# The layer norm's short steps moved off GpSimd, the residual sum as a ScalarE pass, and q weights permuted by their load

## The chip, the cores and the metric

The kernel runs on one core of a Trainium2 chip. The metric is the device time of one launch in microseconds (us); lower is better. Most quoted times are medians of several runs. A run counts as slow when it lies more than 1.5% above the fastest of the same kernel; medians and ranges list all runs. The engines are called PE (TensorE), DVE (VectorE), ACT (ScalarE), POOL (GpSimd) and SP (the sync engine, which here only issues DMAs). The profile counts sixteen DMA engines for the queues of the core.

## The reference

The input is x, 2048 tokens of width 640, in bf16. Cut to what matters:

```python
xn  = (x - mean(x)) / sqrt(var(x) + 1e-5)              # layer norm, per token
q, k, v = split(xn @ wqkv)                             # 32 heads of 20 columns
phi = lambda t: where(t > 0, t + 1, exp(t)) + 1e-6
kv  = phi(k)^T v ; z = sum(phi(k))                     # per head, over all tokens
A   = (phi(q) @ kv) / (phi(q) . z + 1e-6) @ wo
idx = top 8 tokens of xn @ w_r                         # routing
y   = (silu(xn[idx] @ w_gate) * (xn[idx] @ w_up)) @ w_down * sigmoid(r[idx])
out = x + A + xn + scatter_add(idx, y)                 # note the x + xn
```

## The kernel before

The work falls into three stages. In the first, 16 tiles of 128 tokens go through the norm, a transpose (by DMA; the first two tiles by PE), the K projection (`K`, with the router column), `phi` (`PHa`, `PHb`) and the Gram matrix (`G`, xn^T phi(k)). The second computes q, multiplies the weights together and routes eight tokens through the expert block. The third forms the 16 output tiles. The parts that the change and the argument touch, shortened; `...` marks a cut:

```python
def ln_stats(t, part=None):                      # DVE: two halves, then mean and variance
    ... dve.bn_stats(...) ; dve.bn_stats(...) ; dve.bn_aggr(out=mvs[t][:], in_=sts[t][:])

def ln_mid(t, on_act=True):
    ...
    pool.tensor_scalar(out=nm[:], in0=mv[:, 0:1], scalar1=-1.0, ..., op0=ALU.mult)
    act.activation(c[:], XX[:, t, 1, :], AF.Identity, bias=nm[:])          # c = x - mean
    pool.tensor_scalar(out=t2[:], in0=mv[:, 1:2], scalar1=EPS_BF16, ..., op0=ALU.add)
    pool.tensor_tensor(out=s[:], in0=t2[:], in1=halfc[:], op=ALU.pow)      # sqrt(var + eps)

def ln_xn(t):
    dve.reciprocal(sr[:], s[:])
    dve.tensor_scalar(out=XX[:, t, 0, :], in0=c[:], scalar1=sr[:], ..., op0=ALU.mult)

def tr_dma(t):                                   # xn -> xnT, by the DMA engines
    sp.dma_start_transpose(xnT[:, :, t * P : (t + 1) * P], XX[:, t, 0, :])

def xpx(t, eng=None):                            # x + xn in place, read by the outputs
    (eng or pool).tensor_tensor(out=XX[:, t, 1, :], in0=XX[:, t, 1, :], in1=XX[:, t, 0, :], op=ALU.add)

for t in range(T):
    K(t)                                         # PE, reads xnT of tile t
    PHb(t - 1)                                   # DVE: pk = min(ek, 1) + rk
    ln_xn(t + 2) ; tr_dma(t + 2)                 # two tiles ahead
    ln_stats(t + 3)
    if t in dve_extra: perm_q(dve_extra[t])      # two DVE copies, tiles 6 to 10
    PHa(t)                                       # ACT: ek = exp, rk = relu
    ln_mid(t + 3)
    G(t - 1)                                     # PE, reads pk of tile t - 1
    ...
    if 7 <= t: xpx(t)                            # tiles 0 to 6 follow in stage 2
    loads(t)                                     # weights for stages 2 and 3, all on the sync queue
```

`loads` spreads the later weights over the loop: q (0.8 MB) at tiles 4 and 5, o at 6 and 7, gate (2 MB) at 6 to 10, up (2 MB) at 11 to 15, v at 12 and 13; down (2 MB) comes after the loop.

## Time and profile before

| | us |
|---|---|
| median of all runs (lowest, highest) | 143.65 (143.02 to 143.92) |
| span of the profiled run | 142.3 |
| stage 1, to the first q matmul | 72.0 |
| stage 2, from there to the first output matmul | 38.5 |
| stage 3, from there to the end | 31.8 |

The page's busy shares of the kernel before; each row of digits is the span in 40 slices of 3.56 us, in tenths (PEclk is the granted PE clock, DMA the mean busy share of the 16 DMA engines):

```profile
PE 118.6 (83%) x952; PEld 65.5 (46%) x952; DVE 99.7 (70%) x216; ACT 68.8 (48%) x166; POOL 58.6 (41%) x99
PE   6669887887757756669999999894999999999970
POOL 5264468775556775599000047999000000000000
PEclk9977999999999999999999999999689999999999
DMA  4954656695994564398449200000000022222222
```

Counted from 0, PE has its gaps in slices 0 to 17, the stage-1 loop. In slice 27 it pauses and in 28 and 29 it runs at a lower clock, just after POOL worked again (PE is idle from 97.5 to 99.5 us, and its granted clock is 0.50 from 101 to 104 us).

The chain of waits of the kernel before, over one turn of the loop (start us, length us, what):

```profile
43.57 1.24 DVE XX L165
44.81 0.40 DVE stats L138
45.21 0.40 DVE stats L140
45.63 0.22 DVE mv L141
45.93 0.24 POOL nm L152
46.25 0.82 POOL t L157
47.14 0.58 POOL s L158
48.02 1.24 DVE XX L165
```

One tile takes 4.45 us here (43.57 to 48.02). The chain is the norm itself: DVE statistics, three tiny POOL operations, DVE `xn` (L165). PE is not in it. From the groups of instructions (busy us, mean ns of one, idle before and who ended it):

```profile
L184 POOL TENSOR_TENSOR XX<-XX 128x640 bf16<-128x640 bf16 x16 | 25.4, 1612 | 0.0
L476 DVE SCALAR_TENSOR_TENSOR pqT<-qe,qr 128x512 bf16<-128x512 bf16 x20 | 17.2, 870 | 1.1 <-ACT qr L471 1.1
L165 DVE TENSOR_SCALAR XX<-c,sr 128x640 bf16<-128x640 bf16 x16 | 11.4, 712 | 1.6
```

`xn` (L165) takes 0.39 us in the early tiles and 1.24 us from tile 10 on, where the POOL add of x + xn runs beside it. And the transposes, from the view of the tile `xnT`:

```profile
L181 SPq DMA_TRANSPOSE xnT<-XX x14: 1206/1212/1320, 10.7 to 62.4; - x14
DMA to landing us min/median/max: 2.6/3.1/3.6
```

A transpose lands about 3.1 us after its issue starts. The profile can match only some landings to their issues (5 of the 14 here). Where that matters below, I use the time from the start of a transpose's issue to the first K matmul that reads it, which the timeline gives for every tile.

### The profile page before, as it was taken

The numbers are of one execution on the slowest core, as the hardware profiler recorded it, in microseconds if no ns is written. First come the engines' busy times: TensorE is split into PE (matmuls) and PEld (weight loads), VectorE is DVE, ScalarE is ACT, GpSimd is POOL, SyncE is SP. The second block draws the span as 40 slices with busy tenths as digits, with TensorE's granted clock in tenths as the row PEclk, the third lists the DMA queues.
The fourth block names the chain that finished last, engine by engine and source line by source line (L and its number), as shares of the span: only waits on it lengthen the run. The fifth ranks groups of instructions, "written<-read, shape, count | busy, mean of one in ns | idle before, by whom it ended". The sixth has DMA issues, their size and how long they took to land.

```text
span 142.3 us, 2672 instructions
## 1 busy us (share of the span) xinstructions
PE 118.6 (83%) x952; PEld 65.5 (46%) x952; DVE 99.7 (70%) x216; ACT 68.8 (48%) x166; POOL 58.6 (41%) x99
## 2 busy tenths in 40 slices
PE   6669887887757756669999999894999999999970
PEld 2245544444434433335646555341454655566640
DVE  1976664667797776786486787999779595764551
ACT  3068564667633663483286499586456601300000
POOL 5264468775556775599000047999000000000000
PEclk9977999999999999999999999999689999999999
DMA  4954656695994564398449200000000022222222
GB/s 103 314 183 89 170 132 87 162 214 129 264 256 133 150 157 107 95 275 268 180 83 377 92 13 9 0 0 0 7 0 0 5 92 94 92 97 92 92 92 92
DMA packets 20517, 17.06 MB, mean 120 GB/s; under 512 B 10896, under 2 KB 19224, under 8 KB 20504
## 3 DMA queue, kind: packets, MB, share of 16 engines
q1 hardware_dynamic: 19176, 16.07, 40.6%
q10 hardware_dynamic: 1328, 0.82, 2.0%
q8 instruction: 7, 0.11, 0.3%
q14 instruction: 6, 0.05, 0.1%
HBM read 11.80 MB, written 2.62 MB: 101 GB/s over the span
## 4 chain that ended last, share of the span: by engine, by line
PE 44%; DVE 27%; POOL 17%; issue 5%; DMA 2%; ACT 1%; DVEq 1%; POOLq 0%
PE PS L672 16%; PE PS L464 11%; DVE XX L165 8%; POOL s L158 6%; POOL t L157 5%; POOL nm L152 4%; DVE stats L140 4%; DVE stats L138 4%; DVE pqT L476 3%; PE PS L225 2%; DVE mv L141 2%; DMA XX<-in_A_x_dram 2%; PE PS L680 2%; DVE sr L164 2%; DVE pk L220 1%
## 5 line engine op out<-in xcount | busy, mean ns | idle before, releaser
L225 PE MATMUL PS<-pk,XX 128*128 128x512 bf16 x80 | 23.4, 378 | 10.2 <-DVE pk L220 10.2
L195 PE MATMUL PS<-wk,xnT 128*128 128x320 bf16 (+1 forms) x160 | 25.9, 310 | 3.4 <-DMA xnT<-XX 1.7
L184 POOL TENSOR_TENSOR XX<-XX 128x640 bf16<-128x640 bf16 x16 | 25.4, 1612 | 0.0
L464 PE MATMUL PS<-xnT,wqp 128*128 128x512 bf16 x100 | 24.9, 385 | 0.0
L672 PE MATMUL PS<-Mb,pqT 128*128 128x320 bf16 x160 | 24.1, 300 | 0.0
L153 ACT ACTIVATE c<-XX,nm 128x640 bf16<-128x640 bf16 x15 | 12.4, 828 | 21.8 <-POOL nm L152 21.5
L195 PEld LDWEIGHTS <-xnT 128*128 128x128 bf16 x160 | 15.8, 101 | 12.6 <-DMA xnT<-XX 3.3
L686 DVE TENSOR_TENSOR o<-PS,XX 128x640 bf16<-128x640 f32 x16 | 12.8, 820 | 10.9 <-PE PS L680 6.5
L672 PEld LDWEIGHTS <-pqT 128*128 128x128 bf16 x160 | 14.7, 98 | 7.2 <-issue 0.4
L476 DVE SCALAR_TENSOR_TENSOR pqT<-qe,qr 128x512 bf16<-128x512 bf16 x20 | 17.2, 870 | 1.1 <-ACT qr L471 1.1
L470 ACT ACTIVATE qe<-PS 128x512 bf16<-128x512 f32 x20 | 12.0, 599 | 9.9 <-PE PS L464 8.6
L220 DVE SCALAR_TENSOR_TENSOR pk<-ek,rk 128x640 bf16<-128x640 bf16 x16 | 15.1, 946 | 2.0 <-ACT rk L214 2.0
L213 ACT ACTIVATE ek<-PS 128x320 bf16<-128x320 f32 x32 | 13.7, 429 | 4.4 <-PE PS L195 4.4
L230 PE MATMUL PS<-pk,XX 128*128 128x128 bf16 x64 | 14.0, 218 | 0.0
L214 ACT ACTIVATE rk<-PS 128x320 bf16<-128x320 f32 x32 | 14.0, 436 | 0.0
L464 PEld LDWEIGHTS <-wqp 128*128 128x128 bf16 x100 | 9.1, 99 | 9.8 <-issue 1.5
L152 POOL TENSOR_SCALAR nm<-mv 128x1 f32<-128x1 bf16 x15 | 6.1, 403 | 18.0 <-DVE mv L141 17.8
L165 DVE TENSOR_SCALAR XX<-c,sr 128x640 bf16<-128x640 bf16 x16 | 11.4, 712 | 1.6
L230 PEld LDWEIGHTS <-XX 128*128 128x128 bf16 x64 | 6.2, 97 | 12.9 <-issue 12.7
L471 ACT ACTIVATE qr<-PS 128x512 bf16<-128x512 f32 x20 | 11.9, 594 | 0.0
L225 PEld LDWEIGHTS <-XX 128*128 128x128 bf16 x80 | 7.8, 97 | 8.4 <-issue 0.3
L164 DVE RECIPROCAL sr<-s 128x1 f32<-128x1 bf16 x16 | 2.6, 163 | 12.9 <-POOL s L158 12.8
(131 smaller groups left out, 139.7 us busy)
## 6 DMA issues: line engine op xcount, KB each, us to landing
out_dram<-o SPq DMA_DIRECT2D x16, 160.0 KB, 1.8
wg<-in_B_w_gate_dram SPq DMA_DIRECT2D x5, 384.0 KB, 4.0
wu<-in_B_w_up_dram SPq DMA_DIRECT2D x5, 384.0 KB, 3.6
wd<-in_B_w_down_dram SPq DMA_DIRECT2D x1, 1920.0 KB, 7.8
XX<-in_A_x_dram SPq DMA_DIRECT2D x4, 320.0 KB, 3.2
XX<-in_A_x_dram SPq DMA_DIRECT2D x4, 160.0 KB
XX<-in_A_x_dram SPq DMA_DIRECT2D x1, 640.0 KB, 7.0
wk<-in_A_wqkv_dram ACTq DMA_DIRECT2D x1, 480.0 KB, 5.7
```

What stands on the lines that cost most here:

```text
L165: dve.tensor_scalar(out=XX[:, t, 0, :], in0=c[:], scalar1=sr[:], scalar2=None, op0=ALU.mult)
L184: (eng or pool).tensor_tensor(out=XX[:, t, 1, :], in0=XX[:, t, 1, :], in1=XX[:, t, 0, :], op=ALU.add)
L195: pe.matmul(PS[:, 6 + h, 0:w], lhsT=xnT[:, kc, t * P : (t + 1) * P], rhs=wk[:, kc, h * HW : h * HW + w], start=(kc == 0), stop=(kc == KC - 1),
L213: act.activation(ek[:, sl], PS[:, 6 + h, 0:HW], AF.Exp)
L214: act.activation(rk[:, sl], PS[:, 6 + h, 0:HW], AF.Relu)
L220: dve.scalar_tensor_tensor(out=pk[:, t, :], in0=ek[:], scalar=1.0, in1=rk[:], op0=ALU.min, op1=ALU.add)
L225: pe.matmul(PS[:, a, :], lhsT=lhsT, rhs=pk[:, t, 0:512], start=(t == 0), stop=(t == T - 1),)
L230: pe.matmul(PS[:, 5, a * P : (a + 1) * P], lhsT=lhsT, rhs=pk[:, t, 512:D], start=(t == 0 and a == 0), stop=(t == T - 1), skip_group_check= ...
L464: pe.matmul(PS[:, bank, :], lhsT=wqp[:, kc, m, :], rhs=xnT[:, kc, tb * TBLK : (tb + 1) * TBLK], start=(kc == 0), stop=(kc == KC - 1),)
L476: dve.scalar_tensor_tensor(out=pqT[:, m, tb * TBLK : (tb + 1) * TBLK], in0=e, scalar=1.0, in1=r, op0=ALU.min, op1=ALU.add,)
L672: pe.matmul(PS[:, b + h, 0:HW], lhsT=pqT[:, kc, t * P : (t + 1) * P], rhs=Mb[:, kc, h * HW : (h + 1) * HW], start=(first and kc == 0), sto ...
L686: dve.tensor_tensor(out=o[:].rearrange("p (h c) -> p h c", h=2), in0=PS[:, b : b + 2, 0:HW], in1=XX[:, t, 1, :].rearrange("p (h c) -> p h ...
```

## The change

The intent is to take the norm's short POOL steps off the loop's chain and to end the quarrel of POOL and DVE. GpSimd keeps one `pow` per tile. The adds of x and xn become `(1 + sr) x - m sr` on ScalarE in the output stage, where it has time (busy 4.5 of the 32 us before). The q weights arrive already permuted, by a load with pieces of 240 and 16 bytes, which saves ten DVE copies. Loads in the loop move from the sync queue to ScalarE's. The diff, cut to its core:

```diff
 def ln_mid(t, on_act=True):
+    dve.tensor_scalar(out=t2[:], in0=MV[:, t, 1:2], scalar1=EPS_BF16, scalar2=None, op0=ALU.add)
+    pool.tensor_tensor(out=s[:], in0=t2[:], in1=halfc[:], op=ALU.pow)
     if on_act:
-        pool.tensor_scalar(out=nm[:], in0=mv[:, 0:1], scalar1=-1.0, scalar2=None, op0=ALU.mult)
-        act.activation(c[:], XX[:, t, 1, :], AF.Identity, bias=nm[:])
+        act.activation(c[:], XX[:, t, 1, :], AF.Identity, bias=MV[:, t, 0:1], scale=-1.0)
...
-    pool.tensor_scalar(out=t2[:], in0=mv[:, 1:2], scalar1=EPS_BF16, scalar2=None, op0=ALU.add)
-    pool.tensor_tensor(out=s[:], in0=t2[:], in1=halfc[:], op=ALU.pow)
...
-def xpx(t, eng=None):
-    (eng or pool).tensor_tensor(out=XX[:, t, 1, :], in0=XX[:, t, 1, :], in1=XX[:, t, 0, :], op=ALU.add)
+def xpx_cols():
+    dve.tensor_scalar(out=SR1[:], in0=SR[:], scalar1=1.0, scalar2=None, op0=ALU.add)
+    dve.scalar_tensor_tensor(out=MR[:], in0=MV[:, :, 0], scalar=-1.0, in1=SR[:], op0=ALU.mult, op1=ALU.mult)
+def xpx(t):
+    act.activation(XX[:, t, 1, :], XX[:, t, 1, :], AF.Identity, bias=MR[:, t : t + 1], scale=SR1[:, t : t + 1])
...
-def perm_q(kc): ...                                      # two DVE copies per row block
+def wqld(k0, k1):
+    for kc in range(k0, k1):
+        ld(act, wqp[:, kc, :, 0:HB], wqkv_v[:, kc, 0 : KC * HB].rearrange("p (m c) -> p m c", c=HB))
+        ld(act, wqp[:, kc, :, HB:P], wqkv_v[:, kc, KC * HB : D].rearrange("p (m c) -> p m c", c=8))
 def loads(t):
-    if t == 4: ld(sp, wq[:, 0:3, :], ...)
-    if t == 5: ld(sp, wq[:, 3:KC, :], ...)
-    if t == 6: ld(sp, wo[:, 0:3, :], ...)
-    if t == 7: ld(sp, wo[:, 3:KC, :], ...) ; ld(sp, woe[:], ...)
+    if 4 <= t < 9: wqld(t - 4, t - 3)
+    if t == 9: ld(act, wo[:, 0:3, :], ...)
+    if t == 10: ld(act, wo[:, 3:KC, :], ...) ; ld(act, woe[:], ...)
     if 6 <= t < 11:
-        ld(sp, wg[:, t - 6, :], wg_v[:, t - 6, :])
+        ld(act, wg[:, t - 6, :], wg_v[:, t - 6, :])
...                                                       # up and v: sp -> act, same tiles
```

Also in it: the k weights go to the sync queue and tile 1 of x to ScalarE's; the head constants are made before the loop; the statistics are ordered half a tile earlier; the `xpx` passes are strewn over the output stage.

More of the change, by code (lines that the diff above doesn't have):

```diff
@@ L69 @@
     wk = st([P, KC, D + 1], BF16, "wk", "wkM")
-    wq = st([P, KC, D], BF16, "wq", "wqv")
     wqp = st([P, KC, KC, P], BF16, "wqp")
     wo = st([HB, KC, D], BF16, "wo")
+    wv = st([P, KC, D], BF16, "wv")
     woe = st([ED, D], BF16, "woe")
@@ L88 @@
     rbf = st([P, T], BF16, "rbf")
+    MV = st([P, T, 2], BF16, "MV")
+    SR = st([P, T], F32, "SR")
+    SR1 = st([P, T], F32, "SR1")
+    MR = st([P, T], F32, "MR")
     def ld(eng, dst, src):
@@ L96 @@
     dve.memset(zero[:], 0.0)
-    ld(act, wk[:, 0:2, 0:D], wqkv_v[:, 0:2, D : 2 * D])
-    ld(act, wk[:, 2:KC, 0:D], wqkv_v[:, 2:KC, D : 2 * D])
+    ld(sp, wk[:, 0:2, 0:D], wqkv_v[:, 0:2, D : 2 * D])
+    ld(act, XX[:, 1, 1, :], x_v[:, 1, :])
+    ld(sp, wk[:, 2:KC, 0:D], wqkv_v[:, 2:KC, D : 2 * D])
     with nc.allow_non_contiguous_dma(reason="one column"):
         ld(act, wk[:, :, D : D + 1], B_w_r.rearrange("(kc p o) -> p kc o", p=P, o=1))
-    for t in range(1, 4):
+    for t in range(2, 4):
         ld(sp, XX[:, t, 1, :], x_v[:, t, :])
@@ L121, in tok @@
                   allow_small_or_imprecise_dtypes=True)
-    tok(0, 1280)
     dve.memset(one11[:], 1.0)
@@ L126, with ln_stats @@
     dve.memset(eps6[:], 1e-6)
-    mvs = {}
     sts = {}
-    def ln_stats(t, part=None):
-        if part != 1:
+    def ln_stats(t, part):
+        if part == 0:
             stats = tmp.tile([P, 2, nc.vector.BN_STATS_DIM], F32, tag="stats", name="stats")
-            mv = tmp.tile([P, 2], BF16, tag="mv", name="mv", bufs=4)
-            mvs[t] = mv
             sts[t] = stats
             dve.bn_stats(out=stats[:, 0, :], in_=XX[:, t, 1, 0:320])
-        if part != 0:
+        else:
             dve.bn_stats(out=sts[t][:, 1, :], in_=XX[:, t, 1, 320:D])
-            dve.bn_aggr(out=mvs[t][:], in_=sts[t][:])
+            dve.bn_aggr(out=MV[:, t, :], in_=sts[t][:])
     cs = {}
     def ln_mid(t, on_act=True):
-        mv = mvs[t]
-        nm = tmp.tile([P, 1], F32, tag="nm", name="nm", bufs=4)
         t2 = tmp.tile([P, 1], BF16, tag="t2", name="t2", bufs=4)
@@ L150, in ln_mid @@
         c = tmp.tile([P, D], BF16, tag="c", name="c", bufs=3)
+        dve.tensor_scalar(out=t2[:], in0=MV[:, t, 1:2], scalar1=EPS_BF16, scalar2=None, op0=ALU.add)
+        pool.tensor_tensor(out=s[:], in0=t2[:], in1=halfc[:], op=ALU.pow)
         if on_act:
-            pool.tensor_scalar(out=nm[:], in0=mv[:, 0:1], scalar1=-1.0, scalar2=None, op0=ALU.mult)
-            act.activation(c[:], XX[:, t, 1, :], AF.Identity, bias=nm[:])
-        else:
-            dve.tensor_scalar(out=nm[:], in0=mv[:, 0:1], scalar1=1.0, scalar2=None, op0=ALU.mult)
-            dve.tensor_scalar(out=c[:], in0=XX[:, t, 1, :], scalar1=nm[:], scalar2=None, op0=ALU.subtract)
-        pool.tensor_scalar(out=t2[:], in0=mv[:, 1:2], scalar1=EPS_BF16, scalar2=None, op0=ALU.add)
-        pool.tensor_tensor(out=s[:], in0=t2[:], in1=halfc[:], op=ALU.pow)
+            act.activation(c[:], XX[:, t, 1, :], AF.Identity, bias=MV[:, t, 0:1], scale=-1.0)
+        else:
+            nm = tmp.tile([P, 1], F32, tag="nm", name="nm", bufs=2)
+            dve.tensor_scalar(out=nm[:], in0=MV[:, t, 0:1], scalar1=1.0, scalar2=None, op0=ALU.mult)
+            dve.tensor_scalar(out=c[:], in0=XX[:, t, 1, :], scalar1=nm[:], scalar2=-1.0,
+                              op0=ALU.subtract, op1=ALU.mult)
         cs[t] = (c, s)
@@ L162, in ln_xn @@
         c, s = cs[t]
-        sr = tmp.tile([P, 1], F32, tag="sr", name="sr")
-        dve.reciprocal(sr[:], s[:])
-        dve.tensor_scalar(out=XX[:, t, 0, :], in0=c[:], scalar1=sr[:], scalar2=None, op0=ALU.mult)
+        dve.reciprocal(SR[:, t : t + 1], s[:])
+        dve.tensor_scalar(out=XX[:, t, 0, :], in0=c[:], scalar1=SR[:, t : t + 1], scalar2=-1.0,
+                          op0=ALU.mult, op1=ALU.mult)
     def tr_pe(t, b0, b1, eng=None):
@@ L214, in PHa, with rcopy @@
             act.activation(rk[:, sl], PS[:, 6 + h, 0:HW], AF.Relu)
-        if 1 in hs:
-            act.copy(rbf[:, t : t + 1], PS[:, 7, HW : HW + 1])
+    def rcopy(t):
+        act.copy(rbf[:, t : t + 1], PS[:, 7, HW : HW + 1])
     def PHb(t):
@@ L255, in zround @@
             )
-    ln_stats(0)
-    ln_mid(0, False)
-    ln_stats(1, 0)
-    ln_xn(0)
-    ln_stats(1, 1)
-    tr_pe(0, 0, 1, act)
-    ln_mid(1)
-    ln_stats(2)
-    ln_xn(1)
     def consts_a():
@@ L311, in consts_d @@
         pool.iota(lowkey[:], pattern=[[-P, T]], base=LOW, channel_multiplier=-1)
-    def perm_q(kc):
-        dve.tensor_copy(
-            wqp[:, kc, :, 0:HB], wq[:, kc, 0 : KC * HB].rearrange("p (m c) -> p m c", c=HB)
-        )
-        dve.tensor_copy(
-            wqp[:, kc, :, HB:P], wq[:, kc, KC * HB : D].rearrange("p (m c) -> p m c", c=8)
-        )
-    pool_extra = {2: consts_a, 3: consts_b, 4: consts_c, 5: lambda: (consts_d(), tok(1280, 1664)), 6: lambda: tok(1664, S)}
-    dve_extra = {6: 0, 7: 1, 8: 2, 9: 3, 10: 4}
+    pool_extra = {1: lambda: tok(0, 512), 2: consts_b, 3: consts_c, 4: lambda: (consts_d(), tok(512, 1024)),
+                  5: lambda: tok(1024, 1536), 6: lambda: tok(1536, S)}
     wo_v = A_wo[0 : KC * HB, :].rearrange("(m p) d -> p m d", p=HB)
@@ L326 @@
     wu_v = B_w_up.rearrange("(kc p) n -> p kc n", p=P)
+    def wqld(k0, k1):
+        with nc.allow_non_contiguous_dma(reason="column blocks"):
+            for kc in range(k0, k1):
+                ld(act, wqp[:, kc, :, 0:HB], wqkv_v[:, kc, 0 : KC * HB].rearrange("p (m c) -> p m c", c=HB))
+                ld(act, wqp[:, kc, :, HB:P], wqkv_v[:, kc, KC * HB : D].rearrange("p (m c) -> p m c", c=8))
     def loads(t):
@@ L330, in loads @@
             ld(sp, XX[:, 8 + 2 * t : 10 + 2 * t, 1, :], x_v[:, 8 + 2 * t : 10 + 2 * t, :])
-        if t == 4:
-            ld(sp, wq[:, 0:3, :], wqkv_v[:, 0:3, 0:D])
-        if t == 5:
-            ld(sp, wq[:, 3:KC, :], wqkv_v[:, 3:KC, 0:D])
-        if t == 6:
-            ld(sp, wo[:, 0:3, :], wo_v[:, 0:3, :])
-        if t == 7:
-            ld(sp, wo[:, 3:KC, :], wo_v[:, 3:KC, :])
-            ld(sp, woe[:], A_wo[KC * HB : D, :])
+        if 4 <= t < 9:
+            wqld(t - 4, t - 3)
+        if t == 9:
+            ld(act, wo[:, 0:3, :], wo_v[:, 0:3, :])
+        if t == 10:
+            ld(act, wo[:, 3:KC, :], wo_v[:, 3:KC, :])
+            ld(act, woe[:], A_wo[KC * HB : D, :])
         if 6 <= t < 11:
-            ld(sp, wg[:, t - 6, :], wg_v[:, t - 6, :])
+            ld(act, wg[:, t - 6, :], wg_v[:, t - 6, :])
         if 11 <= t < 16:
-            ld(sp, wu[:, t - 11, :], wu_v[:, t - 11, :])
+            ld(act, wu[:, t - 11, :], wu_v[:, t - 11, :])
         if t == 12:
-            ld(sp, wv[:, 0:3, :], wqkv_v[:, 0:3, 2 * D : 3 * D])
+            ld(act, wv[:, 0:3, :], wqkv_v[:, 0:3, 2 * D : 3 * D])
         if t == 13:
-            ld(sp, wv[:, 3:KC, :], wqkv_v[:, 3:KC, 2 * D : 3 * D])
+            ld(act, wv[:, 3:KC, :], wqkv_v[:, 3:KC, 2 * D : 3 * D])
+    consts_a()
+    ln_stats(0, 0)
+    ln_stats(0, 1)
+    ln_mid(0, False)
+    ln_stats(1, 0)
+    ln_xn(0)
+    ln_stats(1, 1)
+    tr_pe(0, 0, 1, act)
+    ln_mid(1, False)
+    ln_stats(2, 0)
+    ln_xn(1)
+    ln_stats(2, 1)
     for t in range(T):
@@ L356 @@
             ln_mid(2)
+            ln_stats(3, 0)
             PHa(0, (1,))
-        else:
-            K(t)
-        if t >= PHI_FIRST:
-            PHb(t - 1)
-        if t + 2 < T:
-            ln_xn(t + 2)
-            if t + 2 > PE_TR:
-                tr_dma(t + 2)
-        if 1 <= t < PHI_FIRST:
-            PHb(t - 1)
-        if t + 3 < T:
-            ln_stats(t + 3)
-        if t in dve_extra:
-            perm_q(dve_extra[t])
-        if t > 0:
-            PHa(t)
-        if t + 3 < T:
-            ln_mid(t + 3)
-        if t >= 1:
+            rcopy(0)
+            ln_xn(2)
+            tr_dma(2)
+            PHb(0)
+            ln_stats(3, 1)
+            ln_mid(3)
+            ln_stats(4, 0)
+        else:
+            K(t)
+            if t >= 2:
+                PHb(t - 1)
+            if t + 2 < T:
+                ln_xn(t + 2)
+                tr_dma(t + 2)
+            PHa(t)
+            rcopy(t)
+            if t + 3 < T:
+                ln_stats(t + 3, 1)
+                ln_mid(t + 3)
+            if t + 4 < T:
+                ln_stats(t + 4, 0)
             G(t - 1)
@@ L379 @@
             pool_extra[t]()
-        if 7 <= t:
-            xpx(t)
-        if t == 11:
-            wv = st([P, KC, D], BF16, "wv", "wqv")
         loads(t)
@@ L719 @@
     route2()
-    for t in range(0, 7):
-        xpx(t)
     m_edge(4)
@@ L766 @@
     q_fin(3, 0)
+    xpx_cols()
     q_pe(3, 2, 0)
@@ L776 @@
     den(2, 4)
+    xpx(0)
     out_one(0, 2)
     q_fin(3, 4)
+    xpx(1)
     bcast(2, (4, 5, 6, 7))
@@ L782 @@
     norm(2, 1, 5, dve)
+    xpx(2)
     out_one(1, 0)
@@ L785 @@
     norm(2, 3, 7, dve)
+    xpx(3)
     out_one(2, 2)
@@ L788 @@
     norm4(2, 4)
+    xpx(4)
     out_one(3, 0)
     den(3, 4)
+    xpx(5)
+    xpx(6)
     out_one(4, 2)
@@ L795 @@
     norm(3, 1, 5, dve)
+    xpx(7)
     out_one(6, 2)
@@ L798 @@
     norm(3, 3, 7, dve)
+    for t in range(8, T):
+        xpx(t)
     out_one(7, 0)
```

## The prediction

> **What bounds the kernel now.** The chain of waits splits the 142.3 us span into three stages.
>
> 1. Norm and K/G loop, to about 72 us. The chain runs DVE statistics, POOL `nm`, `t`, `s`, DVE `xn`, and round again: POOL is 17% of the span's chain and the matmul groups hardly appear before 64 us. By the timeline, one tile takes about 3.5 us at 25 to 36 us and 4.4 us from 39 us on, where the POOL add x+xn joins. One tile costs PE only 2.66 us (K 1.36, G 1.30, read at 65.6 to 68.3 us). `xn` takes 0.39 us alone and 1.24 us beside the POOL add.[...] The head constants also hold the chain once, 20.4 to 23.3 us.
> 2. q and kv, 72 to 110 us: mostly PE, except 86 to 100 us, where DVE leads because seven left-over POOL adds stretch `pqT` from 0.68 to 1.83 to 1.88 us. PE then idles 2 us at 97.5 us, and its granted clock is 0.5 from 101 to 104 us.
> 3. Outputs, 110 us to the end: PE, about 1.5 us a tile plus scatter.
>
> **What changes.** Removed from the loop: POOL `nm` and `t` (0.24 us each alone, up to 0.8 when blocked by DVE), 16 POOL adds (25.4 us), ten DVE q permutes (2.9 us). Added: DVE `t2` (about 0.2 us a tile), two column operations (about 0.3 us once). Added in stage 3: 16 ScalarE affine passes. `c` with one pointer operand took 0.83 us, 0.74 back to back[...], on an engine busy 4.5 us of that 32 us stage. Weight loads move to ScalarE's queue at about 0.5 us an issue, up to three a tile; the q load has 640 pieces of 16 bytes and 640 of 240 per row block, which will lengthen the transposes' landing (3.1 us now).
>
> **Sum.** New tile period, estimated from the durations above: DVE 0.77+0.27+0.39+0.82+0.24+0.2 = 2.65 us, ACT 1.27+0.2+0.74 = 2.2 plus issues, PE 2.66. [...]I take 2.9. The fill is unchanged: K of tile 4 starts near 20.6 us (now about 21), so K of tile 15 starts near 52.5 us instead of 65.6: 13 us saved. Stage 2 returns about 3 us: no stretched `pqT`, no half-clock stretch. Stage 3 stays within 0.5 us, as PE sets its pace. 143.6 - 13 - 3 = 127.5 us.
>
> Predicted: 127.5 us; 8 in 10 between 124 and 132.5. Faster by over 2%: 0.96; within 2%: 0.03; slower: 0.01.
>
> **What would show it.** Loop period 2.7 to 3.1 us; `xn` about 0.39 us throughout; POOL nearly gone from the chain; PE leading in the loop's second half; `pqT` mean about 0.7 us (0.87 now); the 101 us half-clock stretch gone; [...]the output stage as long as before.
>
> **What would make it wrong.** The small q descriptors fill the DMA engines, transposes land 5 us or more after issue, and K waits for them at tiles 6 to 10 (period over 3.2). Or load issues block ScalarE's sequencer so that `ek`/`rk` come late. Or the pow still stands between statistics and `xn`. Or the affine passes come after the outputs' accumulation and hold the eviction. Better than said: the three-way balanced loop holds 2.7 us.

Where the text shows a mark, a passage without a trace or run of this case behind it is cut: an explanation of the times of `xn`, an estimate for the affine pass (twice), and the ground for taking 2.9 us a tile. The 2.9 us, against 2.65 and 2.66 us added up, stand as allowance alone; no trace showed the `pow` slowed beside `pk` (571 to 635 ns in the kernel before). The time of the affine pass was no term of the sum, as stage 3 was said to stay within 0.5 us.

Measured figures to the text, from the profile of the kernel before: POOL's `t` took 0.22 us at 27.13 us, where DVE stood idle, and 0.81 us at 46.25 us, where it ended 0.08 us after the `pk` beside it; `c` took 0.83 us, and where another followed at once, the next ScalarE pass began 0.74 us after its start (46.20 to 46.94 us); a load on ScalarE's queue took 0.49 to 0.51 us to issue. The 0.2 us for `t2` and 0.3 us for the column operations are estimates; the nearest pass there, the one-column `sr` on DVE, took 0.16 us. (In the first profile of the kernel after, `t2` took 0.16 us and the two column operations 0.33 us together.)

## The result, and the profile after

The kernel after took 135.74 us (134.09 to 137.65, 4 runs) against 143.65 us; the ratio of the fast runs is 0.942 (95% interval 0.932 to 0.951). A ratio here is the mean time of one kernel's fast runs over that of the other's fast runs of the same rounds, so not quite the ratio of the quoted medians. It is faster, as said, but far from 127.5 us and outside the range of 124 to 132.5 us. The profile taken with these runs was of a slow one. So I ran the kernel again (`r1_after`): 133.89 us (132.70 to 135.85, 6 runs, ratio 0.936), with a fast profiled run of 132.70 us. All lines "after" below are of that run. It came just under the 134 to 137 us expected of it; the late transposes are as expected.

> The changed kernel again, as the control of this batch. Expected 134 to 137 us as before. All theories: transposes land a median of 5 us after issue, with the worst over 7 us in the loop's second half; the first four tiles of the loop, ahead of the weight loads, keep the 2.5 us period.

| stage, us | before | predicted | after |
|---|---|---|---|
| 1, to the first q matmul | 72.0 | 58.9 | 64.7 |
| 2, to the first output matmul | 38.5 | 35.5 | 34.4 |
| 3, to the end | 31.8 | 31.8 | 31.9 |
| span | 142.3 | 126.2 | 131.0 |

The predicted column follows from the prediction: K of tile 15 at 52.5 us plus the 6.4 us that lie between it and the q matmuls before, then minus 3, then no change. Stages 2 and 3 came as said or better. Stage 1 is the miss: it gave 7.3 us in place of 13. Busy shares of the kernel after, in 40 slices of 3.28 us:

```profile
PE 115.0 (88%) x942; PEld 65.4 (50%) x952; DVE 89.2 (68%) x226; ACT 81.1 (62%) x181; POOL 19.4 (15%) x53
PE   6569999589978956899999999999999999999960
POOL 7211157533111121000000044000000000000000
PEclk9965799999999999999999999999999999999999
DMA  4790675996999999985089000000000122212222
```

POOL is nearly gone and the pause and low clock at 97 to 104 us with it (the granted clock is 1.00 from 88 to 99 us, the same part of stage 2). PE now has gaps in slices 7 to 16 (23 to 56 us), and in that stretch the DMA row stands mostly at 9. Groups that answer to those of before:

```profile
L163 DVE TENSOR_SCALAR XX<-c,SR 128x640 bf16<-128x640 bf16 x16 | 6.3, 393 | 1.6
L475 DVE SCALAR_TENSOR_TENSOR pqT<-qe,qr 128x512 bf16<-128x512 bf16 x20 | 13.5, 683 | 1.2 <-ACT qr L470 1.1
L187 ACT ACTIVATE XX<-XX,MR,SR 128x640 bf16<-128x640 bf16 x16 | 13.6, 913 | 0.0
```

`xn` takes 0.39 us in the mean (0.49 at most) and `pqT` 0.68 us. The new ScalarE pass with two pointer operands takes 0.91 us in the mean; `c`, with one, takes 0.85 us in the same profile. The chain of waits after, in the stretch that is slow:

```profile
35.13 0.39 DVE XX L163
35.54 5.71 DMA xnT<-XX
41.30 0.87 PE PS L198 x5
...
44.71 0.39 DVE XX L163
45.12 7.78 DMA xnT<-XX
52.95 1.54 PE PS L198 x10
```

The norm chain of POOL and DVE is gone from here. What stands in its place is the transpose: 5.71 and 7.78 us from the end of `xn` to the K matmul that needs it. The waits by total (us, times, longest), and then the line of landings from the view of the tile `xnT`:

```profile
PEld L198 <- DMA xnT<-XX: 8.6, 6, 2.1
PE PS L198 <- DMA xnT<-XX: 6.6, 6, 1.8
```

```profile
DMA to landing us min/median/max: 3.8/5.6/6.6
```

The same two waits were 3.3 and 1.7 us before, and the median landing was 3.1 us.

### The profile page after: what moved, and what is told of

It is laid out like the page before. It is cut to its first block, busy times and chain, and to the rows that moved or that the text cites. A ratio compares the mean times of both kernels' runs of the same rounds, so it can differ in the third digit from the quotient of the medians.

```text
span 135.9 us, 2664 instructions
## 1 busy us (share of the span) xinstructions
PE 117.4 (86%) x952; PEld 65.9 (49%) x952; DVE 89.2 (66%) x226; ACT 81.2 (60%) x181; POOL 19.4 (14%) x53
## 4 chain that ended last, share of the span: by engine, by line
PE 49%; DMA 23%; DVE 14%; ACT 5%; issue 4%; DVEq 1%; SPq 1%; POOL 0%; ACTq 0%
DMA xnT<-XX 18%; PE PS L463 17%; PE PS L671 13%; DMA XX<-in_A_x_dram 5%; PE PS L198 4%; DVE pk L224 4%; PE PS L229 2%; DVE XX L163 2%; ACT ek L216 2%; DVE stats L140 2%; DVE stats L138 2%; ACT rk L217 1%; PE PS L633 1%; PE PS L679 1%; PE PS L596 1%
## 5 line engine op out<-in xcount | busy, mean ns | idle before, releaser
L198 PE MATMUL PS<-wk,xnT 128*128 128x320 bf16 (+1 forms) x160 | 27.5, 322 | 10.2 <-DMA xnT<-XX 9.1
L229 PE MATMUL PS<-pk,XX 128*128 128x512 bf16 x80 | 24.9, 396 | 0.4 <-DVE pk L224 0.4
L224 DVE SCALAR_TENSOR_TENSOR pk<-ek,rk 128x640 bf16<-128x640 bf16 x16 | 13.1, 820 | 16.4 <-ACT rk L217 16.3
L234 PE MATMUL PS<-pk,XX 128*128 128x128 bf16 x64 | 14.4, 225 | 0.0
L475 DVE SCALAR_TENSOR_TENSOR pqT<-qe,qr 128x512 bf16<-128x512 bf16 x20 | 13.5, 682 | 1.2 <-ACT qr L470 1.1
L187 ACT ACTIVATE XX<-XX,MR,SR 128x640 bf16<-128x640 bf16 x16 | 13.6, 914 | 0.0
L150 POOL TENSOR_TENSOR s<-t,halfc 128x1 bf16<-128x1 bf16 x16 | 8.9, 554 | 33.2 <-DVE t L149 29.8
L152 ACT ACTIVATE c<-XX,MV 128x640 bf16<-128x640 bf16 x14 | 11.9, 852 | 2.3 <-DVE MV L141 2.2
L229 PEld LDWEIGHTS <-XX 128*128 128x128 bf16 x80 | 8.1, 102 | 9.3 <-issue 1.6
L138 DVE BATCH_NORM_STATS2 stats<-XX 128x6 f32<-128x320 bf16 x16 | 7.8, 485 | 3.6 <-DMA XX<-in_A_x_dram 3.6
L521 DVE TENSOR_TENSOR pqT<-PS,pqT 128x512 bf16<-128x512 f32 x12 | 7.7, 682 | 1.2 <-PE PS L500 1.2
L140 DVE BATCH_NORM_STATS2 stats<-XX 128x6 f32<-128x320 bf16 x16 | 7.8, 485 | 0.0
```

The costliest lines, as they stand in the source:

```text
L187: act.activation(XX[:, t, 1, :], XX[:, t, 1, :], AF.Identity, bias=MR[:, t : t + 1], scale=SR1[:, t : t + 1])
L198: pe.matmul(PS[:, 6 + h, 0:w], lhsT=xnT[:, kc, t * P : (t + 1) * P], rhs=wk[:, kc, h * HW : h * HW + w], start=(kc == 0), stop=(kc == KC - 1),
L224: dve.scalar_tensor_tensor(out=pk[:, t, :], in0=ek[:], scalar=1.0, in1=rk[:], op0=ALU.min, op1=ALU.add)
L229: pe.matmul(PS[:, a, :], lhsT=lhsT, rhs=pk[:, t, 0:512], start=(t == 0), stop=(t == T - 1),)
L234: pe.matmul(PS[:, 5, a * P : (a + 1) * P], lhsT=lhsT, rhs=pk[:, t, 512:D], start=(t == 0 and a == 0), stop=(t == T - 1), skip_group_check= ...
L475: dve.scalar_tensor_tensor(out=pqT[:, m, tb * TBLK : (tb + 1) * TBLK], in0=e, scalar=1.0, in1=r, op0=ALU.min, op1=ALU.add,)
```

## The experiments

**How much time a transpose has.** The table is read from the timelines: the start of K of each tile, and under it the time from the start of the tile's transpose issue to that K. The last pair of rows is the kernel `r14_best` of the end of this section, whose loop stands still almost nowhere.

| tile | 5 | 6 | 7 | 8 | 9 | 10 | 11 | 12 | 13 | 14 | 15 |
|---|---|---|---|---|---|---|---|---|---|---|---|
| before: K starts | 25.16 | 29.15 | 32.47 | 35.83 | 40.23 | 43.88 | 48.34 | 52.79 | 57.09 | 61.40 | 65.61 |
| after: K starts | 25.69 | 29.04 | 31.72 | 34.39 | 37.88 | 41.30 | 43.97 | 48.34 | 52.95 | 55.63 | 58.30 |
| after: issue to K | 3.88 | 4.58 | 5.96 | 4.87 | 5.01 | 5.75 | 5.46 | 6.63 | 7.83 | 7.84 | 6.13 |
| `r14_best`: K starts | 24.59 | 27.26 | 29.93 | 32.60 | 35.27 | 37.94 | 40.60 | 43.27 | 45.94 | 48.61 | 51.28 |
| `r14_best`: issue to K | 4.56 | 4.60 | 4.75 | 4.18 | 4.18 | 4.19 | 4.18 | 4.19 | 4.19 | 4.18 | 4.19 |

The undisturbed loop turns once in 2.67 us, which is just PE's own work for one tile (K 1.36, G 1.30). At that pace a transpose is issued 4.19 us before it is needed. One that lands later makes PE wait, and PE, being the bound, never gets that time back. After, the loop lost 0.6 us a tile in the mean ((58.30 - 25.69) / 10 = 3.26 us).

In the first round I set three theories against each other: the small pieces of the q load fill the DMA engines ("pieces"); the weight loads as such, now packed into a shorter loop, delay the transposes ("loads"); or issuing them from ScalarE's queue is at fault ("queue"). The expectations split "loads" in two: "sum" (all DMA work together, small pieces included) and "bulk" (only the large weight loads). Later ones add "fetch" (PE's instruction fetches) and "mixing" (a fetch, a load and a transpose together).

**1. The plain q load back, all else as after (`r2_plainq`).** The core of the edit:

```diff
-        if 4 <= t < 9:
-            wqld(t - 4, t - 3)
+        if t == 4:
+            ld(act, wq[:, 0:3, :], wqkv_v[:, 0:3, 0:D])
+        if t == 5:
+            ld(act, wq[:, 3:KC, :], wqkv_v[:, 3:KC, 0:D])
+            if t in dve_extra:                           # tiles 6 to 10, ten DVE copies
+                perm_q(dve_extra[t])
```

> The changed kernel, with only the q load undone: two plain loads and ten DVE permutes in the loop (2.9 us of DVE). Theory pieces (the 16 and 240 byte pieces alone made the transposes late): landing median back to 3.1 to 3.5 us, 127 to 129 us. Theory sum (all DMA work that the shorter loop has to hold[...]): 129 to 132 us, with late transposes still in the second half, where the gate and up weights load. Theory bulk (only the large weight loads matter): 134 us or more, as DVE is longer.

Measured: 134.62 us (133.59 to 135.75), ratio 0.940, against 133.89 us and 0.936 for the kernel after of the same rounds. Nothing is gained; the number is in the range of "bulk", and the median landing is 4.6 us, not the 3.1 to 3.5 us that "pieces" asked for. The theory "pieces" falls, and with it the reason that the prediction gave for late transposes. The packet records show how much the pieces cost: in the kernel after, 3200 pieces of 16 bytes took 9 ns each and as many of 240 bytes 23 ns (means), so (9 + 23) ns x 3200 / 16 = 6.4 us of each engine; here 640 rows of 1280 bytes at 75 ns (mean; the median is 55) cost 3.0 us. That is about 3.4 us more, spread over five tiles, and less than I had expected.

**2. Gate, up and down out of the loop (`r3_latew`).**

```diff
-        if 6 <= t < 11:
-            ld(act, wg[:, t - 6, :], wg_v[:, t - 6, :])
-        if 11 <= t < 16:
-            ld(act, wu[:, t - 11, :], wu_v[:, t - 11, :])
...                                      # both after the loop; down after the routing row
```

> The changed kernel, q load kept in pieces, with the ten gate and up weight loads (3.9 MB, about 11 us of all engines at the 350 GB/s seen) issued after the loop, and the down weights after the routing row. Theory pieces: no gain, 134 to 136 us, transposes still 5 us. Theory sum: 128 to 131 us, transposes late at tiles 5 to 9 only. Theory bulk: 127 to 128 us and no late transposes.

(Its 350 GB/s are near the busiest slices of the pages: 377 GB/s in the kernel before and 332 GB/s in the first profile of the kernel after, both in slice 21. The 11 us are 3.9 MB at that rate.)

Measured: 131.87 us (131.34 to 132.21), ratio 0.921. It gains 2 us, which lies in none of the ranges that I had written: less than "sum" (128 to 131 us) or "bulk" asked for, more than "pieces" allowed. In its timeline tiles 7 to 10 run at 2.67 us, and then a gap of 6.2 us stands between two tiles, where the o loads (and, see experiment 13, an instruction fetch) meet a transpose: 7.73 us from issue to K at tile 11. A second gap, of 3.75 us, stands at tile 14. So the loads do matter, but fewer bytes did not remove single long waits.

**3. The same loads on the sync queue, as before the change (`r4_spq`).**

```diff
-            ld(act, wo[:, 0:3, :], wo_v[:, 0:3, :])
+            ld(sp, wo[:, 0:3, :], wo_v[:, 0:3, :])
...                                      # likewise q, o, gate, up and v
```

> The changed kernel with the loop's loads issued from the sync queue, as before the change, instead of ScalarE's. Theory queue (the second queue's packets take turns with the transposes, and that made them late): landing back to near 3.1 us, 130 us or less. Theory sum or pieces (the engines are full, whichever queue feeds them): within 2 us of the control. Theory ScalarE issue (issuing holds up the evictions): 2 us or more faster than the control, with ScalarE waiting less for TensorE.

Measured: 133.33 us (133.10 to 133.56), ratio 0.933, within the spread of the kernel after; its late tiles wait as well (7.11 us from issue to K at tile 12). "Queue" falls.

**4. No weight load at all during the loop (`r5_noload`).** All of them are issued after tile 15, so the q stage has to wait for them and the total must be bad; only the loop is to be read.

```diff
+            if t == T - 1:
+                wqld(0, KC)
+                ld(act, wv[:], ...) ; ld(act, wo[:], ...) ; ld(act, woe[:], ...)
...                                      # then gate and up; down after the routing row
```

> The changed kernel with every load of the loop's tiles 4 to 15 (q, o, v, gate, up) issued only after the last tile; the q stage then has to wait for them, so the loop is what is read, not the total. In all runs so far the pk instructions stand 2.5 to 2.7 us apart, except gaps just after TensorE's 16 KB instruction fetches near 22.5 and 43 to 46 us. Theory sum (DMA work of the loads): no gap over 2.8 us from tile 1 to tile 13, pk of tile 14 about 33.5 us after pk of tile 1 (41.6 in the control). Theory fetch (a fetch beside transposes stalls the engines): a gap of 1.3 us above the period near 24 us and 2 us or more near 45 us remain, 37 us or more.

Measured: 144.94 us in total (2 runs). From tile 6 to tile 15 the loop is what "loads" asked for: K starts every 2.67 us without one wait. Its rows (40 slices of 3.55 us) show the quiet loop in slices 8 to 14 with the DMA engines mostly at 2 tenths, and then PE waiting for weights, at half its clock; the line of landings follows:

```profile
PE   6759798799999999500029999999999999999970
PEclk9986999999999999995555999999999999999999
DMA  4771567822262214989999594000000022222222
```

```profile
DMA to landing us min/median/max: 2.6/2.7/3.4
```

So the weight loads beside the transposes are the cause of the late gaps. One early gap stays: 3.8 us between the `pk` of tiles 4 and 5, where only loads of x and of constants run. Because of it `pk` of tile 14 comes 35.5 us after that of tile 1, between the 33.5 us of the one theory and the 37 us of the other.

**5. Is it PE's instruction fetch? (`r6_shift`).** In the trace, 16 KB packets on the instruction queue start at 22.1, 45.6 and 62.8 us, near gaps. (Some expectations place them a few tenths of a us later than the starts that I give here.) Between two of these packets lie 241 to 274 of PE's records. Forty more tiny matmuls at the start are to bring them earlier.

```diff
-    warm(10)
+    warm(6)
+    for _ in range(44):
+        pe.matmul(PS[:, 7, 0:16], lhsT=zero[:, 0:P], rhs=zero[:, 0:16], start=True, stop=True)
```

> The changed kernel with 6 long and 44 very short warm-up matmuls in place of 10 long ones: 80 more TensorE instructions[...]: near 17, 40 and 56 us instead of 22.5, 46 and 63. Theory fetch: the gap from pk 4 to pk 5 (3.9 us) moves to about pk 2 or 3, near 18 us, and the gaps at pk 12 and 13 move to about pk 10. Theory sum: the gaps stay at tiles 5, 12 and 13, where the loads are. Total 133 to 136 us by either, as a gap only moves.

(The cut clause gave a reason for a shift of two tiles or 5.3 us; the times after it are those expected of the fetches.)

Measured: 133.84 us, ratio 0.934, no change of the total. The fetches moved to 14.4, 38.1 and 62.4 us. An early gap stayed, and the gaps at tiles 12 and 13 moved to tiles 10 and 11, but the largest one, 5.70 us, stands at tile 15 (K at 61.24 us), before the fetch at 62.4 us. Mixed, and its profiled run was a slow one. In `r5_noload` a fetch at 40.8 us made no gap, so there a fetch alone did no harm.

**6. Seven adds of x + xn back on GpSimd in stage 2 (`r7_pooladd`).** This tests the part of the prediction that seemed right.

```diff
+    for t in range(0, 7):
+        pool.tensor_tensor(out=XX[:, t, 1, :], in0=XX[:, t, 1, :], in1=XX[:, t, 0, :], op=ALU.add)
```

> The changed kernel with the first seven x+xn additions back on GpSimd after the routing gathers, as before the change (the other nine stay affine passes of ScalarE). [...]pqT stretched to 1.3 us and more while they run, TensorE idle some 2 us, perhaps a half-clock stretch after it, stage 2 longer by 2 to 4 us, total 136 to 138 us. If stage 2's gain came from elsewhere: unchanged, 134 us.

Measured: 137.97 us (136.54 to 138.74), ratio 0.956 against 0.935 for a neighbour without the adds (experiment 7). Stage 2 grew from 34.4 to 37.2 us (it is 34.4 us in the slow profiled run of experiment 7 too), and the group of `pqT` shows it:

```profile
L480 DVE SCALAR_TENSOR_TENSOR pqT<-qe,qr 128x512 bf16<-128x512 bf16 x20 | 16.7, 842 | 1.1 <-ACT qr L475 1.1
```

842 ns against 683, and 1.88 us at most. The profiled run was slow, but the fast runs (136.54 and 137.33 us) carry the same verdict. What makes `pqT` longer while the adds run is not shown, only that it is. The seven adds cost 2.8 us of stage 2, near the 3 us predicted. The stretch of half clock did not come back with them: PE was idle for 1.7 of the 4 us from 92 to 96 us, and its granted clock stayed at 1.00 from 88 to 104 us (in the kernel before it was 0.50 from 101 us on, 1.5 us after a pause of 2.0 us).

**7. Tile 2 of x ahead of the k weights (`r8_fill`).**

```diff
     ld(act, XX[:, 1, 1, :], x_v[:, 1, :])
+    ld(act, XX[:, 2, 1, :], x_v[:, 2, :])
     ld(sp, wk[:, 2:KC, 0:D], ...)
```

> The changed kernel with x tile 2 loaded by ScalarE's queue ahead of the second part of the k weights, instead of behind them on the sync queue. The first statistics of tile 2 stood at 8.96 us, waiting 1.0 us for that load. If the fill is on the chain: tile 2 about 1 us sooner, total 0.5 to 1.2 us less. If the loop's gaps absorb it: no change.

Measured: 133.85 us, ratio 0.935. The loop begins 0.8 us earlier (first `pk` at 11.53 in place of 12.33 us) and the total does not move: in its profiled run, a slow one, later waits for transposes take the gain back. A gain ahead of a wait that something else sets is no gain.

**8. o, v, gate and up together at tile 14, the head-constant copies apart, and the fill of experiment 7 (`r9_late`).** By then every transpose is issued.

```diff
+        if t == T - 2:
+            ld(sp, wv[:], ...) ; ld(sp, wo[:], ...) ; ld(sp, woe[:], ...)
+            ld(sp, wg[:], ...) ; ld(sp, wu[:], ...)
...                                      # removed from tiles 6 to 15; down after the routing row
+        if 5 <= t < 8:                  # one copy per tile, in place of three at tile 2
+            ld(sp, hmp[32 * (t - 4) : 32 * (t - 4) + 32, :, :], hmp[0:32, :, :])
```

> The changed kernel with three edits: o, v, gate and up weights issued by the sync queue from tile 14 on (the q pieces stay in tiles 4 to 8), the down weights after the routing row; the three hmp copies one at a time in tiles 5 to 7 instead of together at tile 2; x tile 2 ahead of the k weights' second part. Theory sum and mixing (loads that share the engines with the transposes make K wait): pk at 2.5 to 2.7 us from tile 1 to tile 15, first q matmul near 57 to 59 us (64.7 in the control), total 125 to 129 us. If the gaps come from something else: first q matmul 62 us or later, total 131 us or more.

Measured: 128.84 us (127.51 to 130.39), ratio 0.898. From tile 7 the loop runs at 2.67 us to its end, and the first q matmul starts at 57.6 us, a little before the 58.9 us predicted for the change itself. But stage 2 grew to 36.4 us. The chain of waits names one piece:

```profile
60.36 8.09 DMA krow<-c
```

This is the row of routing keys, half a kilobyte, on the sync queue behind the gate and up weights. In the kernel after it took 5.4 us; where up and down were issued after it, 1.7 and 2.2 us (experiment 11) or 3.2 us (`r14_best`).

**9. The head-constant copies apart, alone (`r10_hmp`).** In the kernel after, three copies and an x load hold the sync queue from 19.17 to 21.70 us, and the transpose of tile 5 has to wait behind them until 21.80 us, though its `xn` ended at 20.4. (The three copies took 1.89 us to issue and the x load 0.59 us; most transposes take 1.2 us.)

```diff
-        for j in range(1, 4):            # consts_b, tile 2
-            ld(sp, hmp[32 * j : 32 * j + 32, :, :], hmp[0:32, :, :])
...                                       # one per tile at tiles 5 to 7, as above
```

> The changed kernel, with only the three hmp copies spread over tiles 5 to 7. At tile 2 they hold the sync queue's issue for 1.9 us, just before the transpose of tile 5, which is issued at 21.8 us though its xn ends near 20.4. If that makes the early gap: pk 4 to pk 5 falls from 3.9 to 2.8 us or less. If it is the fetch at 22.5 us or the x loads: 3.5 us or more. Total 0 to 1.5 us less than the control, as the later gaps can absorb it.

Measured: 133.94 us, ratio 0.931, no change of the total. The transpose of tile 5 is issued at 20.52 us, and the early gap shrinks from 3.94 to 3.22 us between two `pk`, about half of what it has over 2.67. The rest is taken up in experiment 13.

**10. As experiment 8, but the o load back at tiles 9 and 10 (`r11_late_wo`).**

> As r9_late, but the o weights (0.8 MB in three DMAs, 2.4 us of the engines) stay in tiles 9 and 10, where TensorE's instruction fetch near 42 us falls. Theory mixing (fetch, plain load and transpose together clog the engines): one gap of 2 us or more over the period at pk 10 to 12 comes back, total 1.5 to 4 us over r9_late. Theory sum alone (0.8 MB fits easily into the loop): no gap, same total as r9_late within 0.5 us.

(Its 2.4 us are an estimate: 640 rows of 1280 bytes at 55 ns, the median, to 65 ns, the mean in the first profile of the kernel after, make 2.2 to 2.6 us on each of 16 engines.)

Measured: 128.77 us (128.39 to 131.26), ratio 0.900. One load of 0.8 MB brings the gap back: 5.41 us between the `pk` of tiles 10 and 11, with 6.91 us from issue to K at tile 11, and the q matmuls start at 60.5 in place of 57.6 us. The total is the same as in experiment 8, which I had not expected: with the o load out of the way, the routing row waited less and stage 2 was 34.4 us again.

**11. o at tile 12, v at 13, gate at 14, up and down after the routing row (`r12_late2`); the same with the fetch moved there (`r13_late2_fetch`).** The edit of the second to the first:

```diff
-    warm(10)
+    for _ in range(108):
+        pe.matmul(PS[:, 7, 0:16], lhsT=zero[:, 0:P], rhs=zero[:, 0:16], start=True, stop=True)
```

> As r9_late, but the o weights at tile 12, the v weights at tile 13 and the gate weights at tile 14, all after TensorE's instruction fetch near 40.4 us and before the next, and the up weights only after the routing row, which in r9_late waited 8.1 us behind them. If a plain load beside transposes is harmless without a fetch: no gap over 2.8 us after pk 5, first q matmul 57 to 58.5 us, stage 2 back to 34.5 us from 36.4, total 126 to 127.5 us. If the o load alone clogs the transposes: a gap of 2 us or more over the period at pk 12 to 15, total 128 to 130 us.

> As r12_late2, with 108 very short warm-up matmuls in place of 10 long ones: 196 more TensorE instructions, so that a fetch falls near 45 to 46 us, beside the o load and the transposes of tiles 14 and 15 (and the one near 40.4 us moves to 26 to 27 us, beside the q pieces). Theory mixing (fetch, load and transpose together): a gap of 2 us or more over the period at pk 12 to 15, perhaps one near 27 to 32 us too. If the fetch plays no part: pk as in r12_late2, shifted by the start alone, which may be up to 2 us later.

Measured: 128.00 us (127.03 to 129.82), ratio 0.893, and 128.52 us (128.26 to 130.66), ratio 0.898. In the first, all tiles from 9 to 14 have their 4.19 us, and one gap stands at tile 15. The o load was issued at 46.04 us, the transpose of tile 15 at 47.46; the chain shows what K waited for:

```profile
47.46 6.11 DMA xnT<-XX
```

6.15 us from issue to K instead of 4.19, so 2.0 us lost, with no instruction fetch beside it. With a fetch put near it (44.9 us, before the load began) the gap is the same, 6.05 us. So a plain load alone can cost 2 us, and this gap owes nothing to a fetch. The early gap, however, moved from tile 5 to tile 7 when the early fetch moved from 21.9 to 26.9 us.

**12. All of it put together: o, v and gate at tile 14, up and down after the routing row, copies apart, fill ahead (`r14_best`); with the plain q load (`r15_best_plainq`); and the same move of loads in the kernel before (`r16_before_late`).** The edit of the first to experiment 8, and that of the last to the kernel before:

```diff
-            ld(sp, wu[:], wu_v[:])       # tile 14
     route1()
+    ld(sp, wu[:], wu_v[:])
     ld(sp, wd[:], B_w_down.rearrange("(fc p) n -> p fc n", p=P))
```

```diff
+        if t == T - 2:
+            ld(sp, wv[:], ...) ; ld(sp, wo[:], ...) ; ld(sp, woe[:], ...) ; ld(sp, wg[:], ...)
...                                      # removed from tiles 6 to 15; up and down after route1()
```

> As r9_late (o, v and gate weights behind the last transpose), but the up weights only after the routing row. Theory: K stalls only when a transpose lands more than about 4 us after issue, and no load is left to make it so after tile 8; and the 2 us that r9_late's stage 2 lost were the routing row behind the up weights. pk at 2.7 us to tile 15, first q matmul 57.5 us, stage 2 34.5 us (36.4 in r9_late), total 126 to 127.5 us. If stage 2 stays at 36 us, the row was not it.

> As r14_best, with the q load undone (two plain loads, ten DVE permutes of 2.9 us in all at tiles 6 to 10). If the q pieces harm the transposes even in the quiet loop: faster by 0.5 us or more. If they are cheap (in the control's trace all ten piece loads come to some 6 us of the engines, against 2.4 for the plain ones) and DVE has no 0.58 us to spare in a 2.67 us period: period about 3.0 us at tiles 6 to 10, total 1 to 2 us more.

> The kernel before, with the same loads moved out of its loop as in r14_best. Theory: its loop ran at 3.5 to 4.4 us a tile for GpSimd's sake, transposes landed 3.1 us after issue, so the loads cost it nothing: first q matmul at 72 us within 0.7, total within 1 us of before. If the loads had already held its loop: 2 us or more faster.

| kernel | us, median (range) | ratio to before (95%) |
|---|---|---|
| before, same rounds | 143.72 (142.71 to 144.21) | |
| `r14_best` | 125.25 (124.51 to 125.92) | 0.873 (0.869 to 0.877) |
| `r15_best_plainq` | 126.90 (125.48 to 127.94) | 0.881 (0.876 to 0.887) |
| `r16_before_late` | 142.95 (142.46 to 143.30) | 0.997 (0.991 to 1.002) |

`r14_best` beats both kernels: 18 us off the kernel before. Its rows (40 slices of 3.10 us), its line of landings, and three pieces of its chain of waits:

```profile
PE   5569789799999999999999999999999999999950
DMA  3980568998862633999889980000001122112222
```

```profile
DMA to landing us min/median/max: 2.6/2.8/3.2
```

```profile
35.43 1.36 PE PS L198 x10
36.80 0.22 PE PS L229
37.07 0.22 PE PS L229
```

PE is at 9 from slice 8 on, the DMA engines are least busy in the loop's second half (slices 11 to 15), and the chain of the loop is PE alone. Spans by stage are 57.7, 34.4 and 32.0 us. The total is below the 126 to 127.5 us expected.

The permuted q load, which the prediction feared, does no harm in the quiet loop: from tile 5 on, no tile exceeds PE's pace. By the medians it gains 1.65 us (126.90 - 125.25), though the intervals of the two ratios just touch. `r15_best_plainq` loses in two places (its profiled run was a slow one, so the sizes are rough). Its ten DVE copies stretch tiles 7 to 10 to 2.98 us. And at tile 6 K waits for a transpose beside which the two plain q loads ran (issued at 23.43 and 25.95 us), with no group of slow packets like those of experiment 13:

```profile
22.69 6.21 DMA xnT<-XX
```

K of tile 6 starts at 28.95 us there and at 27.26 us in `r14_best`; that is most of the 2.2 us by which the loop ends later. So it seems that 0.8 MB in two plain loads held a transpose up, where the same bytes in pieces, spread over five tiles, did not; the copies are not all that the pieces save. And the same move of loads does nothing for the kernel before: its loop turned once in 4.05 us ((65.61 - 25.16) / 10), bound by the norm, and its transposes had time. The loads cost nothing until the loop was short.

**13. What makes the longest single waits (`r17_wo_fetch`, `r18_best_fetch`).** In the packet records, packets of 256 bytes are the transposes'; most take about 18 ns. In the 20 profiles I looked for those over 1 us. There are 17 groups of 15 or more, in 15 profiles, and each starts within 1 us of the start of an instruction fetch (from 0.55 us before it to 0.93 us after); a smaller group of 9, in `r6_shift`, has no fetch near. Where a fetch met no bulk load (40.8 us in `r5_noload`, 39.6 us in `r14_best`) there is no group. But a fetch beside loads does not always make one: there is none at 22.1 us in `r1_after` or at 43.5 us in `r4_spq`. So two more runs: experiment 10 with its fetches moved off the o load (the edit of experiment 11), and `r14_best` with its fetches moved earlier (the edit of experiment 5).

> The kernel r11_late_wo with the instruction fetches moved by about 5 us (to about 27 and 45 us, in place of 21.5 and 40.8), so that none falls on the o load at 38 to 43 us. If a long wait needs a fetch, a load and a transpose together: no group of 256-byte packets over 1 us at 40 to 43 us, tile 11 has at most 5.2 us from issue to K in place of 6.91, the gap of 5.4 us between the pk of tiles 10 and 11 shrinks below 3.7, the q matmuls start at 57.5 to 59 us. If the load alone does it: 6.5 us or more from issue to K at tile 11, or at a tile next to it, and q starts near 60.5 us. The total may stay near 128.8 us in both, as stage 2 took the gain back before.

> The kernel r14_best with the instruction fetches moved about 7 us earlier at first (to about 14, 38 and 62 us, in place of 22.1, 39.6 and 59.1). If the fetch makes the early gap: no group of slow packets at 22 us, K of tile 5 starts 2.7 us after that of tile 4 (3.67 in r14_best), the loop ends 0.7 to 1.0 us sooner, 124.3 to 124.8 us. If the x loads in flight do it, or the start of the loop: K of tile 5 again 3.5 us or more after tile 4, and 125.0 to 125.7 us.

| | experiment 10 | `r17_wo_fetch` | `r14_best` | `r18_best_fetch` |
|---|---|---|---|---|
| fetches start, us | 21.5, 40.8 | 25.7, 46.1 | 22.1, 39.6 | 13.8, 33.5 |
| groups of slow packets, us | 22.3, 41.2 | 26.6 | 22.7 | none |
| K of tile 4 to 5, 5 to 6 | 3.79, 2.81 | 2.66, 4.74 | 3.67, 2.67 | 2.67, 3.02 |
| `pk` of tile 10 to 11 | 5.41 | 4.01 | 2.67 | 2.66 |
| first q matmul starts | 60.5 | 59.8 | 57.7 | 57.7 |
| ratio to before, same rounds | 0.900 | 0.893 | 0.873 | 0.879 |
| us, median (range) | 128.77 (128.39 to 131.26) | 128.16 (127.25 to 128.47) | 125.25 (124.51 to 125.92) | 126.01 (125.80 to 126.17) |

In these four kernels the early group of slow packets goes with the fetch, and the early gap goes with both: at tile 5 with the fetch at 21.5 or 22.1 us, at tile 6 with 25.7, gone from tile 5 with 13.8. At the o load the gap shrank by 1.4 us (5.41 to 4.01) when the fetch was taken away, and 1.3 us over the quiet 2.67 stayed. That lies between what I had written for the two theories, so by these profiles, one of each kernel, both have a share: the load alone, and a fetch that meets load and transpose. A fetch is not needed for a long wait: tile 12 of `r4_spq` (7.11 us from issue to K) has no slow packets, and tile 15 of `r10_hmp` (6.68 us) has no fetch near. Moving the fetch brought nothing in the total of `r18_best_fetch`: the early gap was gone from tile 5, 0.35 us came at tile 6, and at tile 10, next to the new fetch at 33.5 us and the last q loads, K waited 0.84 us. The fetches were moved here, not removed: the one at 33.5 us met the last q loads, where the one at 39.6 us in `r14_best` met no bulk load.

## Why the prediction was right or wrong

**Right: what bounded the loop, and that the change removes it.** POOL is off the chain, its busy time falls from 58.6 to 19.4 us, `xn` takes 0.39 us in the mean, and the `pow` is no obstacle (0.55 us in the mean; `SR` waits for it 0.5 us in all). The estimated tile period of 2.9 us was even cautious; undisturbed it is 2.67 us, PE's own work.

**Right: stages 2 and 3.** Stage 2 gave 4.1 us (3 said) with `pqT` at 0.68 us and the stretch of half clock at 101 us gone. Experiment 6 confirms the cause for 2.8 us of it; the rest was not taken apart. Stage 3 stayed at 31.9 us, with the affine pass at 0.91 us.

**Wrong: the term of the transposes' landing, which the sum left at zero.** The prediction says that the q load in pieces "will lengthen the transposes' landing (3.1 us now)", and then adds up a tile from engine times only: "I take 2.9. [...] so K of tile 15 starts near 52.5 us". It started at 58.30 us: 0.7 us of the difference was there at tile 4 (21.29 us, 20.6 said), 5.1 us came in the eleven tiles after it, at 3.36 us each. The step that failed is this: I did not ask how late a transpose may land in the shorter loop. The answer was in the durations: at PE's pace of 2.67 us there are 4.19 us from issue to need, the 3.1 us of before leave one microsecond of slack, and the loop's weights were to pass through the same engines in less time (from K of tile 5 to K of tile 15, 26.7 us undisturbed, 40.4 before). The transposes then took up to 7.8 us from issue to K, and the period became 3.26 us. From K of tile 5 to K of tile 15 that is 32.61 us in place of 26.69 in `r14_best`, so 5.9 us lost; another 1.1 us was lost before tile 5, in the fill and the early gap. Together they are the 7.0 us by which the q matmuls start later than in `r14_best` (64.68 against 57.66).

**Wrong: the suspect.** The prediction named this risk ("transposes land 5 us or more after issue") but blamed "the small q descriptors". Experiments 1 and 12 acquit them: undoing them alone gained nothing, and in the quiet loop they are if anything a gain. (Experiment 1 alone would not do: the plain load in their place makes tile 6 wait too, 5.41 us from issue to K against 4.58.) The loads of o, v, gate and up were at fault, 5.6 MB in all. Shown by: no loads, no late gap (experiment 4); o alone brings one gap back (10, 11), in experiment 10 perhaps half of it with the help of an instruction fetch (13, one profile each); all of them moved, 133.89 to 125.25 us, in ratios to the kernel before 0.936 to 0.873 (12). Part of the last step is the fill and the copies, which gained nothing alone (7, 9), and the routing row ahead of up and down (8).

**So the 127.5 us were within reach of the change,** and slightly beaten, but only with the loads placed for the new loop.

**Open.** What happens inside the DMA engines when a fetch, plain packets and a transpose meet: the records show about 20 of the transposes' packets at 1 us or more, in `r3_latew` from 42.3 to 43.3 us with a median of 1.7 us. They tie this to the fetch by its time, also where the fetch was moved; they tell neither the mechanism nor why some fetches beside loads do nothing of the kind. Why one plain load of 0.8 MB delays one transpose by 1.3 to 2 us and another not at all is open too.

## What to carry to other kernels

When a change shortens a loop, write down for each prefetch how long before its need it is issued in the new loop, and compare that with the time it takes while the other DMAs run; a load that was free in the slow loop can become the bound of the fast one (moving the loads gave the kernel before a ratio of 0.997, and took the kernel after from 0.936 to 0.873). Put bulk loads where no latency-critical transfer is in flight, and small urgent transfers ahead of bulk ones: here that was worth nearly as much as the change itself (133.89 to 125.25 us, after 143.65 to 133.89). A suspicion about the unusual part (the small pieces) is to be tested before it is believed; the ordinary part (plain weight loads) was to blame.
